# Second layer of a two-layer kernel: block-end sums on VectorE or preset in banks instead of on GpSimd, nine places for split inputs, first copies in another order

## The chip, the cores and the metric

The kernel runs on one core of a Trainium2 chip. The metric is the device time of one execution in microseconds (us). A core has a matrix engine (TensorE, PE in the rows), VectorE (DVE), ScalarE (ACT), GpSimd (POOL) and SyncE (SP), which here only starts DMA transfers. Each engine works through its own list in order, and waits on semaphores for the others.

## The reference, cut to what matters

```python
# q, k, v: (4, 8, 576, 64)
scores = scale * np.matmul(q, k.transpose(0, 1, 3, 2))
ret = scores * Dmat[None, :, :, :]              # decay by distance, zero above the diagonal
x = np.matmul(ret, v)                           # then (2304 tokens, 512)
# layer 1: w_in (512, 2048), w_out (2048, 512)
h = x @ w_in
x = (h * np.cos(h)) @ w_out
# layer 2: the same sizes
h = x @ w_in
g = np.where(h >= 1, h, np.where(h <= -1, 0.0, (h + 1) ** 2 / 4.0))
out = (g @ w_out).astype(np.float32)
```

The change touches the second layer, and the last three steps of the first.

## The kernel before, in words

**Tiling.** A float32 operand is split into a rounded high part and the rest, and a product is three passes over these parts (PASSES). The second layer also saves products: each of its two matrix products is cut into 2 by 2 pieces, and seven products of sums of pieces stand in for eight. The 2304 tokens come in three super-blocks of 768 (SB), two halves of 384 (TH). For each super-block there are four steps (NKB), each with a quarter of the 2048 hidden columns, so n counts 12 steps. A step has seven products for h (function products, and product for one) and then, one step later, seven groups for the output (function groups). A product or a group is 12 matmuls of 384 columns in two ops of 6, so a step has 168; the weights of one are one tile of 512 KB, loaded on SP's queue into a ring (function weight).

**Inputs.** The output of layer 1 lies in DRAM (yd). For a super-block, load_inputs fetches four quarter tiles q0 to q3. sum_q makes sums of them in place and in a fifth tile, and split_q makes the seven split inputs xc: ScalarE copies the high part, VectorE subtracts for the low part. In the order rows the tiles q0, q1, q2, q3 are q_4972, q_4974, q_4976, q_4978, and the fifth is q_5071. For the first super-block five of the seven are split while layer 1 still runs (EARLY), the other two after it (XEARLY). There are seven places for xc, one for each product, so the next super-block's copy waits for the last use of that product's place.

**PSUM.** Four double banks T0 to T3 (bkT in rows, pair_bank). Product 1 goes to T0; ScalarE copies T0 into T1 (seed, ACT bkT<-bkT), since products 6, 7 and 4 add to it there. T0 takes the place of layer 1's h banks, T1 that of its banks S and O. VectorE and ScalarE then make the curve g of what the banks hold, four combinations of the results (SUMS2), and seven splits into gh (ScalarE) and gl (VectorE, LOWS). A group's bank is added into an SBUF tile acc (DVE a<-bkT,a); in a super-block's first step ScalarE copies it there instead. The group at list index 5 of GPRODS (SEEDED) has, in all steps but the first, its acc copied into its bank first by ScalarE, and copied back after.

**Block end.** After the four steps of a super-block seven acc tiles are summed into four outputs and stored: six sums on GpSimd and one on VectorE (in the last super-block three and four).

**What sets the order.** The second layer's ops are listed with an engine, a cost, a position and their dependencies (op), and listed() plans the order of every engine's list: PE keeps the written order; every other engine takes, among the ops that are ready within 0.15 us of its earliest, the one of the lowest position. PE's planned clock starts at 0 and those of the other engines at -60, and a load is planned to land 6 us after it starts. So an op that needs nothing of the second layer's PE is planned before time 0, whatever its position. What is planned is fixed: an engine can't pass over an op that waits.

**Names.** In products, ORDER is the order of a step's products on PE (G: the first group of the step before). FIRST is the first step's: L0 and L1 are the last two parts of layer 1 (steps 78 and 79, mm2) and N is the next step's product 1. mm1 is layer 1's first matrix product, mm2 its second; a mm1 of 12 matmuls of 512 columns goes to a bank h, S or O.

Of the kernel before, what the change touches and what calls it, by code (L numbers as in the profile page):

```python
# [33 lines left out]
GPRODS = (1, 4, 2, 7, 5, 6, 3)  # L34
NKB = NQ // 2
EARLY = (0, 2, 3, 1, 4)
XEARLY = {5: 2, 6: 4}
# [5 lines left out]
SEEDED = (5,)  # L43
LOWS = {1: ("DVE", 16.8), 4: ("DVE", 31), 2: ("DVE", 34), 7: ("DVE", 36), 5: ("DVE", 39), 6: ("DVE", 45), 3: ("DVE", 47)}
SUMS2 = {7: ("DVE", 20.4), 5: ("DVE", 21.8), 6: ("DVE", 30), 3: ("DVE", 33)}
XPOS = (-31, -25, -19, -6, -11, 3.6, 1)
# [60 lines left out]
def retention_moe_kernel(ctx: ExitStack, tc: tile.TileContext, qk, kv, win1, wout1, win2, wout2, ktab, out):  # L107
# [490 lines left out]
    def mm1(s):  # L598
# [3 lines left out]
        aside = s - 6 + N1 % 2 if s >= N1 - 2 else s if l == NBLK - 1 and s % 2 and s < N1 - 3 else None  # L602
# [310 lines left out]
    def load_inputs(sb, pos):  # L913
        for j, (h, g) in enumerate(((0, 0), (1, 0), (1, 1), (0, 1))):
            def load(j=j, g=g, o=sb * SB + h * TH):
                if not sb:
                    qa[j][1] = home_early(f"q{j}", (2, TH))
                SY.dma_start(out=qa[j][1], in_=yd[:, 2 * g:2 * g + 2, o:o + TH])
            op("SP", "load", pos + j, load, (), (qa[j][0],))
# [10 lines left out]
    def split_q(eng, pos, k):  # L930
        p = PRODS[k][0]
        if p == 6:
            sum_q(eng, pos - 4, 0, 4, 0, ALU.subtract)
        if p == 3:
            sum_q(eng, pos - 4, 3, 3, 0, ALU.subtract)
        u = qa[{1: 0, 6: 0, 2: 3, 7: 1, 5: 4, 4: 2, 3: 3}[p]]
        hi, lo = ("x", k, 0), ("x", k, 1)
        op("ACT", "copy", pos, lambda: A.activation(xat(k)[:, 0], u[1], AF.Copy), (u[0],), (hi,))
        op("DVE", "wide", pos + 0.8, lambda: V.tensor_tensor(out=xat(k)[:, 1], in0=u[1], in1=f(xat(k)[:, 0]), op=ALU.subtract), (u[0], hi), (lo,))

    def inputs(sb):
        base = sb * NKB * T0
        load_inputs(sb, base - 50)
        sum_q("POOL", base - 40, 4, 1, 2, ALU.add)
        sum_q("POOL", base - 38, 1, 0, 1, ALU.subtract)
        for k, pos in enumerate(XPOS):
            split_q("POOL", base + pos, k)
# [64 lines left out]
    tmp = {t: home2(t, (2, TH)) for t in ("h1", "m5", "u2")}  # L1012
# [3 lines left out]
    def weight(key, src, pos):  # L1016
        n = len(ring)

        def load():
            j = n % 9  # L1020
            pool, tag = (wr, "wi") if j < 5 else (lp, f"w{j - 5}") if j < 7 else (wk, f"wo{j + 7}")
# [3 lines left out]
        ring.append(op("SP", "load", pos, load, (), (("w", n % 9),), ring[-1:]))  # L1025
        return "w", n % 9
# [12 lines left out]
    def product(n, k, b):  # L1039
        sb, kb = n // NKB, n % NKB  # L1040
        p, which, start = PRODS[k]
        which += which == 2 and n == 0
# [315 lines left out]
```

## Time and profile before

| | us |
|---|---|
| three runs | 846.33, 847.08, 850.20 |
| median | 847.08 |
| the profiled execution | 845.47 |
| its span, first to last instruction | 843.7 |
| PE busy | 812.3 (96%) |
| VectorE, ScalarE, GpSimd busy | 656.0, 525.2, 215.6 |
| second layer's first product starts | 466.8 |

The rows come from that one execution. A time of start counts from the span's start. A bracket at the end of a row gives the idle time ahead of the instruction and what ended it. PEclk is the granted TensorE clock as a share of 2.4 GHz; 0.50 is 1.2 GHz.

### The profile page before, as it was taken

The numbers are of one execution on the slowest core, as the hardware profiler recorded it, in microseconds if no ns is written. First come the engines' busy times: TensorE is split into PE (matmuls) and PEld (weight loads), VectorE is DVE, ScalarE is ACT, GpSimd is POOL, SyncE is SP. The second block draws the span as 40 slices with busy tenths as digits, with TensorE's granted clock in tenths as the row PEclk, the third lists the DMA queues.
The fourth block names the chain that finished last, engine by engine and source line by source line (L and its number), as shares of the span: only waits on it lengthen the run. The fifth ranks groups of instructions, "written<-read, shape, count | busy, mean of one in ns | idle before, by whom it ended". The sixth has DMA issues, their size and how long they took to land.

```text
span 843.7 us, 14794 instructions
## 1 busy us (share of the span) xinstructions
PE 812.3 (96%) x5549; PEld 729.5 (86%) x5550; DVE 656.0 (78%) x928; ACT 525.2 (62%) x866; POOL 215.6 (26%) x154
## 2 busy tenths in 40 slices
PE   7999999999999999999999999999999999899996
PEld 5788888887877777778777899999999999899996
DVE  7988787548889898888995475897964897954786
ACT  4788788655665654566656486685565675366560
POOL 2333222423425333324334200021500010500002
PEclk9999999999999999999999999999999999999999
DMA  8997999745989997678885797789878778788772
GB/s 342 393 371 289 347 342 322 275 150 188 318 278 330 327 353 271 229 281 308 324 286 203 257 331 256 252 272 307 265 248 255 252 248 253 250 252 254 256 233 75
DMA packets 78007, 232.92 MB, mean 276 GB/s; under 512 B 8304, under 2 KB 15088, under 8 KB 77936
## 3 DMA queue, kind: packets, MB, share of 16 engines
q1 hardware_dynamic: 77936, 231.98, 79.8%
q8 instruction: 44, 0.72, 0.3%
q14 instruction: 27, 0.22, 0.1%
HBM read 184.76 MB, written 47.19 MB: 275 GB/s over the span
## 4 chain that ended last, share of the span: by engine, by line
PE 38%; DVE 11%; ACT 3%; DMA 2%; issue 2%; POOL 0%; SPq 0%; DVEq 0%; ACTq 0%
PE bkT L124 36%; DVE a L124 3%; DVE gl L124 1%; DMA wq<-cw 1%; DVE cw L288 1%; ACT a L124 1%; DVE t L662 1%; DVE X L271 1%; DVE t L671 1%; PE bkS L608 1%; DMA raw<-in_win_dram 1%; DVE V L272 1%; PE bky L625 0%; DVE s L124 0%; DMA wi<-wd 0%
## 5 line engine op out<-in xcount | busy, mean ns | idle before, releaser
L124 PE MATMUL bkT<-xc,w 128*128 128x384 f32 x1008 | 183.8, 340 | 9.2 <-ACT bkT L124 9.2
L124 PEld LDWEIGHTS bkT<-xc,w 128*128 128x128 f32 x1008 | 179.2, 192 | 10.7 <-ACT bkT L124 10.5
L124 PE MATMUL bkT<-gh,w 128*128 128x384 f32 x672 | 170.4, 334 | 0.0
L608 PE MATMUL h<-xhl,wi 128*128 128x512 f32 (+1 forms) x576 | 139.4, 389 | 2.2 <-DVE t L671 2.1
L608 PEld LDWEIGHTS h<-xhl,wi 128*128 128x128 f32 x576 | 105.5, 188 | 26.4 <-DVE t L671 4.4
L684 POOL TENSOR_TENSOR gl<-t,gh 128x512 fp32r<-128x512 f32 (+1 forms) x57 | 80.7, 1417 | 163.8 <-ACT gh L679 102.2
L124 PEld LDWEIGHTS bkT<-gh,w 128*128 128x128 f32 x672 | 121.2, 188 | 0.0
L124 PE MATMUL bkT<-gl,w 128*128 128x384 f32 x336 | 112.2, 334 | 0.0
L623 PE MATMUL bky<-gh,wo 128*128 128x512 f32 x208 | 82.0, 394 | 0.8 <-ACT gh L679 0.8
L624 PE MATMUL bky<-gh,wo 128*128 128x512 f32 x208 | 81.1, 390 | 0.0
L625 PE MATMUL bky<-gl,wo 128*128 128x512 f32 x208 | 78.1, 393 | 2.5 <-POOL gl L684 2.5
L124 POOL TENSOR_TENSOR a<-a,a 128x768 f32<-128x768 f32 x15 | 34.5, 2302 | 138.7 <-DVE a L124 138.4
L679 ACT ACTIVATE gh<-t 128x512 fp32r<-128x512 f32 (+1 forms) x57 | 35.3, 620 | 54.3 <-DVE t L671 54.1
L124 PEld LDWEIGHTS bkT<-gl,w 128*128 128x128 f32 x336 | 63.1, 188 | 0.0
L124 POOL TENSOR_TENSOR q<-q,q 128x768 f32<-128x768 f32 x8 | 16.0, 2001 | 173.5 <-DVE xc L124 140.6
L124 DVE SCALAR_TENSOR_TENSOR a<-bkT,a 128x768 f32<-128x768 f32 x36 | 34.4, 955 | 31.2 <-ACT a L124 30.7
L124 DVE TENSOR_TENSOR a<-bkT,a 128x768 f32<-128x768 f32 (+1 forms) x55 | 51.4, 938 | 8.6 <-PE bkT L124 8.1
L124 PE MATMUL h<-xhl,wi 128*128 128x256 f32 (+1 forms) x288 | 52.1, 330 | 2.7 <-ACT hs L124 1.7
L666 ACT ACTIVATE t<-t 128x512 f32<-128x512 f32 (+1 forms) x56 | 34.8, 622 | 30.9 <-DVE t L662 30.8
L124 DVE TENSOR_TENSOR gl<-a,gh 128x768 fp32r<-128x768 f32 x48 | 53.1, 1122 | 0.5 <-ACT gh L124 0.5
L124 PEld LDWEIGHTS h<-xhl,wi 128*128 128x128 f32 x288 | 43.7, 189 | 8.6 <-ACT hs L124 1.9
L625 PEld LDWEIGHTS bky<-gl,wo 128*128 128x128 f32 x208 | 38.8, 188 | 12.9 <-POOL gl L684 4.9
(189 smaller groups left out, 1582.3 us busy)
## 6 DMA issues: line engine op xcount, KB each, us to landing
w<-wq SPq DMA_DIRECT2D x84, 512.0 KB, 4.5
w<-wv SPq DMA_DIRECT2D x84, 512.0 KB, 4.4
wi<-wd SPq DMA_DIRECT2D x48, 512.0 KB, 5.3
raw<-in_win_dram SPq DMA_DIRECT2D x32, 512.0 KB, 6.2
raw<-in_wout_dram SPq DMA_DIRECT2D x32, 512.0 KB, 5.3
qkv<-in_qk_dram SPq DMA_DIRECT2D x16, 512.0 KB, 7.7
qkv<-in_kv_dram SPq DMA_DIRECT2D x16, 512.0 KB, 8.6
wd<-wi SPq DMA_DIRECT2D x16, 512.0 KB, 6.2
```

The lines of the kernel that those rows point to most:

```text
L124: ins = fn(*args, **kw)
L271: V.scalar_tensor_tensor(out=X, in0=raw[:, :, 0].bitcast(U32), scalar=2.0 ** -52, in1=X, op0=ALU.mult, op1=ALU.mult)
L272: done.append(V.tensor_tensor(out=v, in0=W, in1=X, op=ALU.add))
L288: V.tensor_tensor(out=t[:, ks, 1], in0=u, in1=f(t)[:, ks, 0], op=ALU.subtract)
L608: lastpe[0] = PE.matmul(hp[s][:, :n], w[:, a, kb, :], x[b][:, kb, :], start=(i == 0), stop=(i == 3 * KB - 1))
L623: PE.matmul(o, w[:, 0, es], a, start=first and e % per == 0, stop=False, skip_group_check=True)
L624: PE.matmul(o, w[:, 1, es], a, start=False, stop=False, skip_group_check=True)
L625: PE.matmul(o, w[:, 0, es], b, start=False, stop=last, skip_group_check=True)
L662: V.scalar_tensor_tensor(out=t, in0=t, scalar=-MAGIC, in1=h, op0=ALU.add, op1=ALU.subtract)
L666: A.activation(u, u, AF.Sin, scale=TWOPI / 2)
L679: A.activation(gh[s], rt[s], AF.Copy)
L684: G.tensor_tensor(out=gl[s], in0=u, in1=f(gh[s]), op=ALU.subtract)
```

## The change

Eight things, all in or just ahead of layer 2:

1. The input sums (sum_q) of the second and third super-block move from GpSimd to VectorE.
2. The block-end sums: of seven, three are now made by presetting a group's bank with another acc (ENDS: groups 6 and 2 with acc 1, group 3 with acc 5; ScalarE, PSUM) and four by VectorE. GpSimd has no work left in layer 2.
3. The groups of products 3, 4 and 5 are preset with their own acc in a super-block's two middle steps, where before that of product 6 was in all steps but the first (SEEDED held list indices, and now holds product numbers); GPRODS and the positions LOWS, SUMS2 are new.
4. xc has nine places used in turn (NX) in place of seven.
5. The weight ring has seven tiles in place of nine: the sixth and seventh were in space of their own and are now where layer 1's last two weights (wo14, wo15) lie.
6. The tile h1 goes; its sum is made in m5's place.
7. The banks of layer 1's last mm1 are dealt otherwise: step 77 in S, 78 in h, 79 in O (before: h, S, S).
8. XPOS, SPOS, XEARLY and the q loads' positions are new.

```diff
@@ -34 +34 @@
-GPRODS = (1, 4, 2, 7, 5, 6, 3)
+GPRODS = (1, 5, 6, 2, 7, 3, 4)
@@ -35,0 +36,2 @@
+NX = 9
+SPOS = (-44, -42)
@@ -37 +39 @@
-XEARLY = {5: 2, 6: 4}
+XEARLY = {5: 6, 6: 8}
@@ -43,4 +45,6 @@
-SEEDED = (5,)
-LOWS = {1: ("DVE", 16.8), 4: ("DVE", 31), 2: ("DVE", 34), 7: ("DVE", 36), 5: ("DVE", 39), 6: ("DVE", 45), 3: ("DVE", 47)}
-SUMS2 = {7: ("DVE", 20.4), 5: ("DVE", 21.8), 6: ("DVE", 30), 3: ("DVE", 33)}
-XPOS = (-31, -25, -19, -6, -11, 3.6, 1)
+SEEDED = (3, 4, 5)
+ENDS = {6: 1, 2: 1, 3: 5}
+SEED_AT = 2
+LOWS = {1: ("DVE", 15), 5: ("DVE", 21), 6: ("DVE", 44), 2: ("DVE", 38.5), 7: ("DVE", 34), 3: ("DVE", 49), 4: ("DVE", 53)}
+SUMS2 = {7: ("DVE", 29), 5: ("DVE", 15), 6: ("DVE", 34), 3: ("DVE", 37.5)}
+XPOS = (-17, -20, -17.5, -4.4, -13, -4.5, -3.2)
@@ -602 +606 @@
-        aside = s - 6 + N1 % 2 if s >= N1 - 2 else s if l == NBLK - 1 and s % 2 and s < N1 - 3 else None
+        aside = None if l < NBLK - 1 else s if s % 2 else s + 1 if s == N1 - 1 else None
@@ -919 +923 @@
-            op("SP", "load", pos + j, load, (), (qa[j][0],))
+            op("SP", "load", pos + 5 * j, load, (), (qa[j][0],))
@@ -930 +934 @@
-    def split_q(eng, pos, k):
+    def split_q(eng, pos, k, sb=0):
@@ -933 +937 @@
-            sum_q(eng, pos - 4, 0, 4, 0, ALU.subtract)
+            sum_q(eng, pos - 2, 0, 4, 0, ALU.subtract)
@@ -935 +939 @@
-            sum_q(eng, pos - 4, 3, 3, 0, ALU.subtract)
+            sum_q(eng, pos - 2, 3, 3, 0, ALU.subtract)
@@ -937,3 +941,4 @@
-        hi, lo = ("x", k, 0), ("x", k, 1)
-        op("ACT", "copy", pos, lambda: A.activation(xat(k)[:, 0], u[1], AF.Copy), (u[0],), (hi,))
-        op("DVE", "wide", pos + 0.8, lambda: V.tensor_tensor(out=xat(k)[:, 1], in0=u[1], in1=f(xat(k)[:, 0]), op=ALU.subtract), (u[0], hi), (lo,))
+        x = (sb * 7 + k) % NX
+        hi, lo = ("x", x, 0), ("x", x, 1)
+        op("ACT", "copy", pos, lambda: A.activation(xat(x)[:, 0], u[1], AF.Copy), (u[0],), (hi,))
+        op("DVE", "wide", pos + 0.8, lambda: V.tensor_tensor(out=xat(x)[:, 1], in0=u[1], in1=f(xat(x)[:, 0]), op=ALU.subtract), (u[0], hi), (lo,))
@@ -943,3 +948,3 @@
-        load_inputs(sb, base - 50)
-        sum_q("POOL", base - 40, 4, 1, 2, ALU.add)
-        sum_q("POOL", base - 38, 1, 0, 1, ALU.subtract)
+        load_inputs(sb, base - 70)
+        sum_q("DVE", base + SPOS[0], 4, 1, 2, ALU.add)
+        sum_q("DVE", base + SPOS[1], 1, 0, 1, ALU.subtract)
@@ -947 +952 @@
-            split_q("POOL", base + pos, k)
+            split_q("DVE", base + pos, k, sb)
@@ -1012 +1017,2 @@
-    tmp = {t: home2(t, (2, TH)) for t in ("h1", "m5", "u2")}
+    tmp = {t: home2(t, (2, TH)) for t in ("m5", "u2")}
+    xplace.update((j, home2(f"xc{j}", (2, 2, TH), F32R)) for j in range(7, NX))
@@ -1020,2 +1026,2 @@
-            j = n % 9
-            pool, tag = (wr, "wi") if j < 5 else (lp, f"w{j - 5}") if j < 7 else (wk, f"wo{j + 7}")
+            j = n % 7
+            pool, tag = (wr, "wi") if j < 5 else (wk, f"wo{j + 9}")
@@ -1025,2 +1031,2 @@
-        ring.append(op("SP", "load", pos, load, (), (("w", n % 9),), ring[-1:]))
-        return "w", n % 9
+        ring.append(op("SP", "load", pos, load, (), (("w", n % 7),), ring[-1:]))
+        return "w", n % 7
@@ -1041,0 +1048 @@
+        x = (sb * 7 + k) % NX
@@ -1051 +1058 @@
-                    PE.matmul(o, w[:, u, h, :], xat(k)[:, v, h, :], start=start and i == h == 0, stop=i == 2 and h == 1, skip_group_check=True)
+                    PE.matmul(o, w[:, u, h, :], xat(x)[:, v, h, :], start=start and i == h == 0, stop=i == 2 and h == 1, skip_group_check=True)
@@ -1053 +1060 @@
-            op("PE", "PE", b + a, lambda a=a: run(a), (key, ("x", k, 0), ("x", k, 1)), (("T", which),))
+            op("PE", "PE", b + a, lambda a=a: run(a), (key, ("x", x, 0), ("x", x, 1)), (("T", which),))
@@ -1062 +1069 @@
-        m5, u2, h1 = [(x, tmp[x]) for x in ("m5", "u2", "h1")]
+        m5, u2 = [(x, tmp[x]) for x in ("m5", "u2")]
@@ -1086 +1093 @@
-                op("PE", "mm2", b + s, lambda j=j: steps_of(N1 - 2 + j, "M"), (("w", 7 + j),), (("last", j),))
+                op("PE", "mm2", b + s, lambda j=j: steps_of(N1 - 2 + j, "M"), (("w", 5 + j),), (("last", j),))
@@ -1108 +1115 @@
-                op("DVE", "wide", b + s - 2, lambda: V.tensor_tensor(out=h1[1], in0=b1[1](), in1=m5[1], op=ALU.add), (m5[0], b1[0]), (h1[0],))
+                op("DVE", "wide", b + s - 2, lambda: V.tensor_tensor(out=m5[1], in0=b1[1](), in1=m5[1], op=ALU.add), (b1[0],), (m5[0],))
@@ -1110 +1117 @@
-                curve(s + 0.6, "a22", h1)
+                curve(s + 0.6, "a22", m5)
@@ -1140,2 +1147,2 @@
-        def sum_of(eng, pos, to, frm):
-            two(eng, pos, (("a", to), acc[to]), (("a", to), acc[to]), (("a", frm), acc[frm]))
+        def sum_of(pos, to, frm):
+            two("DVE", pos, (("a", to), acc[to]), (("a", to), acc[to]), (("a", frm), acc[frm]))
@@ -1153 +1160 @@
-            seeded = kb > 0 and i in SEEDED
+            frm = ENDS[p] if ends and p in ENDS else p if kb and not ends and p in SEEDED else None
@@ -1159 +1166 @@
-                if m == 0 and not seeded:
+                if m == 0 and frm is None:
@@ -1166 +1173 @@
-                        PE.matmul(o, w[:, a, u, m * P:(m + 1) * P], g[:, a], start=not seeded and a == j == 0, stop=a == 1 and j == 2, skip_group_check=True)
+                        PE.matmul(o, w[:, a, u, m * P:(m + 1) * P], g[:, a], start=frm is None and a == j == 0, stop=a == 1 and j == 2, skip_group_check=True)
@@ -1170,3 +1177,5 @@
-                A.activation(bk[tile_][:, :, :TH], c[1], AF.Copy)
-            if seeded:
-                op("ACT", "copy", b - 2, seed, (c[0],), (("T", tile_),))
+                A.activation(bk[tile_][:, :, :TH], acc[frm], AF.Copy)
+            if frm is not None:
+                op("ACT", "copy", b - SEED_AT, seed, (("a", frm),), (("T", tile_),))
+            if ends and p in (7, 4):
+                sum_of(b - 3, p, {7: 6, 4: 7}[p])
@@ -1175 +1184 @@
-            if kb == 0 or seeded:
+            if kb == 0 or frm == p:
@@ -1177 +1186 @@
-            elif lastone and ends and p == 3:
+            elif lastone and ends and p == 4:
@@ -1180 +1189 @@
-                    store(b + 2 + m, 3, 0, 1, slice(m, m + 1))
+                    store(b + 2 + m, 4, 1, 0, slice(m, m + 1))
@@ -1185,3 +1194,2 @@
-            slow = "DVE" if lastone else "POOL"
-            if p == 1:
-                sum_of("POOL", b + 8, 6, 1)
+            if p == 7:
+                sum_of(b + 1, 3, 6)
@@ -1189,13 +1197,10 @@
-                sum_of("POOL", b + 6, 2, 1)
-                store(b + 9, 2, 0, 0)
-            elif p == 5:
-                sum_of("POOL", b + 3, 3, 5)
-            elif p == 6:
-                sum_of("DVE", b + 3, 3, 6)
-                sum_of(slow, b + 3.5, 7, 6)
-                sum_of(slow, b + 4, 4, 7)
-                sum_of(slow, b + 5, 7, 5)
-                store(b + 7, 4, 1, 0)
-                store(b + 8, 7, 1, 1)
-            elif p == 3 and not lastone:
-                store(b + 5, 3, 0, 1)
+                store(b + 4, 2, 0, 0)
+            elif p == 3:
+                store(b + 4, 3, 0, 1)
+                if lastone:
+                    sum_of(b + 3, 5, 7)
+                    store(b + 4, 5, 1, 1)
+            elif p == 4 and not lastone:
+                store(b + 5, 4, 1, 0)
+                sum_of(b + 4, 7, 5)
+                store(b + 7, 7, 1, 1)
```

**ScalarE, start of layer 2.** The rows after the last step of layer 1 (gh). Before, two copies for the first super-block, then the seed of T1:

```order
L679 ACTIVATE gh<-t 128x512
L124 ACTIVATE xc_5482<-q_4976 128x768
L124 ACTIVATE xc_5501<-q_4978 128x768
L124 ACTIVATE bkT_5534<-bkT_5509 128x2x384
L124 ACTIVATE u_5481<-bkT_5534 128x768
```

With the change:

```order
L683 ACTIVATE gh<-t 128x512
L128 ACTIVATE xc_5483<-q_4976 128x768
L128 ACTIVATE xc_5498<-q_4978 128x768
L128 ACTIVATE xc_5481<-q_4972 128x768
L128 ACTIVATE xc_5482<-q_5071 128x768
L128 ACTIVATE bkT_5536<-bkT_5511 128x2x384
L128 ACTIVATE u_5480<-bkT_5536 128x768
```

Two more copies, of q_4972 (q0) and of q_5071 (q1 + q2), stand ahead of the seed; they fill the two added places for the second super-block.

**SP's queue, at the same place.** A load waits for the readers of its tile, and what is behind it waits too. Before, the first step's seven weights, then the second super-block's q tiles:

```order
L124 DMA w_5493<-wq_117 128x1024
L124 DMA w_5495<-wq_118 128x1024
L124 DMA w_5497<-wq_117 128x1024
L124 DMA q_4974<-yd 128x2x384
L124 DMA q_4972<-yd 128x2x384
L124 DMA q_4976<-yd 128x2x384
L124 DMA q_4978<-yd 128x2x384
L124 DMA w_5542<-wq_117 128x1024
```

With the change five weights come first, then the q tiles, then the sixth weight and, behind a store of layer 1's output, the seventh:

```order
L128 DMA w_5494<-wq_117 128x1024
L128 DMA q_4974<-yd 128x2x384
L128 DMA q_4972<-yd 128x2x384
L128 DMA q_4976<-yd 128x2x384
L128 DMA q_4978<-yd 128x2x384
L128 DMA w_5544<-wq_118 128x1024
L128 DMA yd<-a_5478 128x512
L128 DMA w_5573<-wq_117 128x1024
```

The four q loads moved ahead of two weight loads.

**Block end.** In the first super-block GpSimd had six sums in a row (a_5478, a_5477, a_5476, a_5475, a_5474, a_5473, a_5472 are the acc tiles of products 1, 5, 6, 2, 7, 3 and 4 with the change, and of 1, 4, 2, 7, 5, 6 and 3 before):

```order
L124 TENSOR_TENSOR a_5473<-a_5473,a_5478 128x768
L124 TENSOR_TENSOR a_5476<-a_5476,a_5478 128x768
L124 TENSOR_TENSOR a_5472<-a_5472,a_5474 128x768
L124 TENSOR_TENSOR a_5475<-a_5475,a_5473 128x768
L124 TENSOR_TENSOR a_5477<-a_5477,a_5475 128x768
L124 TENSOR_TENSOR a_5475<-a_5475,a_5474 128x768
```

Meanwhile VectorE had low parts, its one sum, and then the last group's bank (a<-bkT):

```order
L124 TENSOR_TENSOR s_5465<-a_5468,s_5466 128x768
L124 TENSOR_TENSOR gl_5455<-a_5468,gh_5462 128x768
L124 TENSOR_TENSOR gl_5454<-a_5469,gh_5461 128x768
L124 TENSOR_TENSOR a_5472<-a_5472,a_5473 128x768
L124 TENSOR_TENSOR a_5472<-bkT_6680,a_5472 128x768
L124 TENSOR_TENSOR gl_5453<-s_5467,gh_5460 128x768
```

With the change (a_5472 is now product 4's, the last group):

```order
L128 TENSOR_TENSOR a_5474<-a_5474,a_5476 128x768
L128 TENSOR_TENSOR gl_5456<-s_5467,gh_5463 128x768
L128 TENSOR_TENSOR a_5475<-bkT_6619,a_5475 128x768
L128 TENSOR_TENSOR a_5473<-a_5473,a_5476 128x768
L128 TENSOR_TENSOR a_5474<-bkT_6648,a_5474 128x768
L128 TENSOR_TENSOR a_5472<-a_5472,a_5474 128x768
L128 TENSOR_TENSOR a_5473<-bkT_6646,a_5473 128x768
L128 TENSOR_TENSOR a_5472<-bkT_6684,a_5472 128x768
L128 TENSOR_TENSOR a_5474<-a_5474,a_5477 128x768
```

VectorE now has the four sums among its banks, and no low part stands between the last two of these.

## Rows read from the trace of the kernel before

**Rows 1.** The page's part 1: span; busy us, share, instructions.

```profile
span 843.7 us, 14794 instructions
PE 812.3 (96%) x5549; PEld 729.5 (86%) x5550; DVE 656.0 (78%) x928; ACT 525.2 (62%) x866; POOL 215.6 (26%) x154
```

**Rows 2.** What PE waited for: us in total, times, longest.

```profile
PE bkT L124 <- ACT bkT L124: 9.2, 3, 3.8
```

**Rows 3.** Timeline, first block end: start, duration, instruction, count, idle before.

```profile
603.42 9.99 POOL L124 TENSOR_TENSOR a<-a,a 128x768 f32<-128x768 f32 x4 [1.76 <-DVE a L124]
...
604.12 2.60 DVE L124 TENSOR_TENSOR gl<-a,gh 128x768 fp32r<-128x768 f32 x1
...
609.17 2.57 DVE L124 TENSOR_TENSOR a<-a,a 128x768 f32<-128x768 f32 x1
611.85 0.96 DVE L124 TENSOR_TENSOR a<-bkT,a 128x768 f32<-128x768 f32 x1
...
613.74 8.07 PE L124 MATMUL bkT<-xc,w 128*128 128x384 f32 x36 [3.85 <-ACT bkT L124]
```

**Rows 4.** Timeline of PE: after the first block end's wait, and at the second.

```profile
621.65 0.51 PE L124 MATMUL bkT<-gh,w 128*128 128x384 f32 x2
...
736.04 8.83 PE L124 MATMUL bkT<-xc,w 128*128 128x384 f32 x36 [3.85 <-ACT bkT L124]
744.71 0.51 PE L124 MATMUL bkT<-gh,w 128*128 128x384 f32 x2
```

**Rows 5.** Busy us by window: PE, PEld, DVE, ACT, POOL, then PEclk, DMA share, GB/s.

```profile
500.00:608.00 108.00, 108.00 (x625) 108.00 (x624) 88.47 (x92) 72.43 (x89) 16.90 (x8) 1.00 0.83 268
...
617.00:618.00 1.00, 1.00 (x5) 1.00 (x4) 0.02 (x1) 0.81 (x1) 0.00 (x0) 0.50 0.89 295
```

**Rows 6.** Timeline of PE where layer 2 starts.

```profile
461.39 0.39 PE L623 MATMUL bky<-gh,wo 128*128 128x512 f32 x1
...
464.12 2.88 PE L608 MATMUL bkS<-xhl,wi 128*128 128x512 f32 x12
...
473.35 2.36 PE L124 MATMUL bkT<-xc,w 128*128 128x384 f32 x12 [1.53 <-ACT bkT L124]
```

**Rows 7.** Timeline of the other engines there; last, q loads from issue to landing.

```profile
471.04 1.56 ACT L124 ACTIVATE xc<-q 128x768 fp32r<-128x768 f32 x2
471.90 2.33 DVE L124 TENSOR_TENSOR xc<-q,xc 128x768 fp32r<-128x768 f32 x2 [0.57 <-ACT xc L124]
472.50 0.79 ACT L124 ACTIVATE bkT<-bkT 128x768 f32<-128x768 f32 x1
...
473.38 1.23 SPq L124 DMA_DIRECT2D q<-yd  x2
...
477.44 3.76 POOL L124 TENSOR_TENSOR q<-q,q 128x768 f32<-128x768 f32 x2 [4.90 <-DMA q<-yd]
...
DMA to landing us min/median/max: 3.9/4.1/5.9
```

**Rows 8.** Groups of instructions, 480 to 600 us: count, busy us, mean ns, idle before.

```profile
L124 DVE TENSOR_TENSOR gl<-a,gh 128x768 fp32r<-128x768 f32 x17 | 15.9, 951 | 0.0
L124 DVE SCALAR_TENSOR_TENSOR a<-h,a 128x768 f32<-128x768 f32 x5 | 6.2, 1246 | 2.8 <-ACT a L124 2.8
L124 ACT ACTIVATE xc<-q 128x768 fp32r<-128x768 f32 x7 | 5.7, 835 | 1.7 <-PE bkT L124 1.7
```

**Rows 9.** Weight loads: count, KB, median us to landing, in 448 to 470 and 480 to 500.

```profile
w<-wq SPq DMA_DIRECT2D x7, 512.0 KB, 4.5
...
w<-wq SPq DMA_DIRECT2D x3, 512.0 KB, 9.0
```

**Rows 10.** Timeline of the tail, PE and VectorE.

```profile
835.34 1.83 DVE L124 TENSOR_TENSOR a<-a,a 128x768 f32<-128x768 f32 x2 [2.03 <-ACT a L124]
836.14 0.34 PE L124 MATMUL bkT<-gl,w 128*128 128x384 f32 x1
...
839.60 0.55 DVE L124 TENSOR_TENSOR a<-bkT,a 128x384 f32<-128x384 f32 x1
```

## The prediction

> **What bounds the kernel now.** I read the page's part 1 first: PE is busy for 96% of the span [rows 1], so an edit elsewhere pays only where it ends a wait of PE, or works after PE's end. Then PE's waits: in layer 2 it waits for one thing, ScalarE's seed of bank T1, three times, 9.2 us in all [rows 2]. The timeline places them: 1.53 us where layer 2 starts [rows 6], and 3.85 us at the ends of the first two super-blocks [rows 3, 4]. The rest of layer 2 has no idle PE: 108.00 of 108.00 us in 500 to 608, 625 matmuls, so 0.1728 us each [rows 5]. Last, the tail: PE ends at 836.14 + 0.34 = 836.48, VectorE at 839.60 + 0.55 = 840.15 [rows 10], the span at 843.7 [rows 1].
>
> **Block ends.** Where the first 3.85 us come from is to be seen in the timeline: four GpSimd sums run from 603.42 for 9.99 us, and a VectorE instruction with two SBUF operands takes 2.60 or 2.57 us under them [rows 3], against 0.951 elsewhere [rows 8]. So VectorE reaches the last group's bank only at 611.85; the seed must wait for that bank, and PE for the seed [rows 3]. The change takes GpSimd out. Three such stretched instructions cost 2.60 + 2.60 + 2.57 - 3 x 0.95 = 4.9 us [rows 3, 8] (the second 2.60 stands between the two shown), more than the wait. What is late next? VectorE gets more to do: by the order, 27 and 26 instructions between the seeds around the first block end (27 and 21 around the second), where GpSimd's were beside 27 and 26. At 0.95 us [rows 8] 27 need 25.7 us; a step of 168 matmuls lasts 29.0 us [rows 5]. Three presets of 0.8 us (as the seed, 0.79 [rows 7]) go to ScalarE, which has at most 30 instructions of some 0.84 [rows 8], 25 us, in such a step. Both fit, so I take both waits as gone.
>
> A wait also costs clock. After the first, 36 matmuls took 621.65 - 613.74 = 7.91 us, after the second 744.71 - 736.04 = 8.67 [rows 3, 4], where 36 x 0.1728 = 6.22; the granted clock was 0.50 in 617 to 618 [rows 5], the lower level, 1.2 GHz. So 1.69 and 2.45 us more. Block ends: -(3.85 + 1.69) - (3.85 + 2.45) = **-11.8 us** (bounds: -11.8, and 0 if VectorE is late anyway, see the rivals).
>
> **Start of layer 2.** Two things change. The last mm1 (step 79) goes to bank O and runs ahead of mm2 of step 77, not after it: 464.12 - 461.39 = 2.73 us earlier [rows 6], and so is all that hangs on it. By itself this would end the 1.53 us wait. But the order shows two more copies ahead of the seed on ScalarE, of q0 and of q1 + q2 for the second super-block, since their places 7 and 8 are free at once. They wait for loads that can't start earlier: q2's tile is read by the first super-block's split, which frees it at 473.38, where SP starts the load [rows 7]; with the change at 473.38 - 2.73 = 470.65. GpSimd's sum, which waited for it, began at 477.44, so it landed in 477.44 - 473.38 = 4.06 us [rows 7]; now at 474.71. Then VectorE's sum (0.95 [rows 8]), ScalarE's copy (0.83 [rows 8]), the seed (0.79) and 0.06 to PE (472.50 + 0.79 against 473.35 [rows 6, 7]): 477.34. PE is done with its work ahead of that at 473.35 - 1.53 = 471.82, as before, since only the order of the same matmuls changes. It waits 5.52 us in place of 1.53: **+4.0 us**. Bounds from the landing: 3.9 us to 5.9 [rows 7], so +3.8 to +5.8; I take the 4.06 of the same load at the same place. VectorE's three instructions more lie in time in which it has nothing else, since its next work needs PE.
>
> The Trainium skill, DMA: Bandwidth & Descriptors, section Anatomy of one DMA, gives (for transfers issued by GpSimd; here SP issues) 2.0 us plus the bytes at 436 GB/s; for 384 KB that is an estimate of 2.9 us, against the 4.06 of the row, and the sum would be 1.2 us lower by it. The row stands in a stretch of busy DMA and decides.
>
> This wait is longer than those of the block ends, so the lower clock should come too: 1.69 to 2.45 us as above, I take the mean, **+2.1**. After the 1.53 us none was lost: the next twelve matmuls took 2.36 us [rows 6].
>
> **Weights.** With seven tiles in place of nine a load starts when the product seven earlier is done, so six products or groups of 12 x 0.1728 = 2.07 us [rows 5], 12.4 us, ahead of its use. It lands in 4.5 us, in 9.0 in the busiest stretch [rows 9]. At the start the sixth and seventh wait for layer 1's last two steps; the seventh then has the four products 2, 5, 7 and N, 8.3 us, to land. I take nothing; bounds 0 and 9.0 - 8.3 = 0.7.
>
> **Last groups.** After the last step PE has seven groups and nothing between. Group 6 is preset from acc 1, so between group 1's end and group 6 VectorE must add 0.95, ScalarE copy 0.8: 1.8 with hand-offs, in the 2.07 us of group 5. If VectorE is in another instruction, up to 0.95 late: 0 to +0.8, **+0.3**.
>
> **Tail.** Before, 3.67 us pass from PE's end to VectorE's, because two pairs of sums (the first 1.83 for two [rows 10]) stand between the halves of the last bank. Now two sums and group 3's bank can run while PE has its last group, and two halves of 0.55 remain: 0.6 to 1.2 us after PE. What follows VectorE's end stays, 843.7 - 840.15 = 3.55. So 4.2 to 4.75 in place of 7.22: -2.5 to -3.0, **-2.6**.
>
> Free: h1 in m5's place (same instructions, m5 isn't written again until a step later), the presets of the middle steps (VectorE adds become ScalarE copies, both off PE's path: ScalarE is 72.43 of 108 us busy [rows 5]).
>
> **Sum.** -11.8 + 4.0 + 2.1 + 0.3 - 2.6 = -8.0 us. The profiled execution took 845.47; 837.5 by it. The median of the runs is 1.6 above it (847.08), so 839.1 for the median.
>
> **Rivals.**
> (a) VectorE is the bound at the block ends. For it: the 27 instructions leave 3 us of a step; the mean of one form in 480 to 600 was 1.25 [rows 8]. It decides from 29.0 / 27 = 1.07 us for the mean instruction: then the last group's bank is late as before. Against: what was stretched there lay under GpSimd. If both waits stay: 847.08 + 4.0 + 2.1 + 0.3 - 2.6 = 850.9, **slower**; if one goes, about 845.
> (b) The start costs nothing: the seed isn't held, because the loads land in time. PE then gains the 1.53 as well: -11.8 - 1.5 + 0.3 - 2.6 = -15.6, 831.5. Against: q2 would have to land by 471.82 - 0.06 - 0.79 - 0.83 - 0.95 = 469.2, before it can start.
> (c) Seven tiles are too few: where loads land later than the 12.4 us, PE waits at each weight; at the start 9.0 us [rows 9] against 8.3 already costs 0.7, with the clock up to 3. 840 to 845.
>
> **How the numbers follow.** My sum 0.68, (a) 0.14 (half of it both waits), (b) 0.06, (c) 0.12. Likeliest: 839.1. Its own range, with landing, clock, last groups and tail at their ends: -11.8 + 3.8 + 1.7 + 0 - 3.0 = -9.3 to -11.8 + 5.8 + 2.5 + 0.8 - 2.5 = -5.2, so 837.8 to 841.9. To hold 8 in 10 it must take in most of (c), one wait of (a) and the runs' own spread (0.75 below the median): 835 to 845.5. About 0.5%, 4.2 us, is what a measurement of this kernel can tell from no change. Faster by more (below 842.9): 0.61 of the sum's 0.68, (b), half of (c): 0.73. Within: 0.07 of the sum, half of (a), a quarter of (c): 0.17. Slower: (a) with both waits, and the part of (c) in which loads are late all through layer 2: 0.10.
>
> **What the profile after would show.** Right: POOL with nothing after layer 1; PE's wait for ACT bkT once, 5 to 6 us, near 472 to 477, with ScalarE's row ahead of the seed waiting for VectorE's q sum, and PEclk 0.50 behind it; no wait of PE at either block end and every gl at 0.95; about 4.5 us from PE's end to the span's. Wrong: PE waiting for ACT bkT at a block end (a), for DMA w (c), or not at all near 472 (b).

## The result, and the profile after

The changed kernel took 837.09 us (median of four, 834.37 to 838.97) against 846.71: a ratio of 0.9875, 95% interval 0.9835 to 0.9916. The profiled execution was the longest of the four, 838.97 us, against 845.47 for that of before; their spans are 837.2 and 843.7.

Busy time (page, part 1), then PE's waits for ScalarE's banks (us in total, times, longest), as [rows 1, 2]:

```profile
span 837.2 us, 14788 instructions
PE 811.9 (97%) x5549; PEld 729.6 (87%) x5550; DVE 642.5 (77%) x933; ACT 543.1 (65%) x893; POOL 166.9 (20%) x131
...
PE bkT L128 <- ACT bkT L128: 5.1, 2, 4.8
```

Three waits of 9.2 us have become one of 4.8 and one of 0.3. The timeline puts the 4.8 where layer 2 starts (as [rows 6, 7]; PE first, then ScalarE, VectorE, SP; last, the q loads from issue to landing):

```profile
463.90 2.88 PE L612 MATMUL bkO<-xhl,wi 128*128 128x512 f32 x12
...
469.35 2.24 PE L128 MATMUL bkT<-xc,w 128*128 128x384 f32 x12
...
479.13 4.21 PE L128 MATMUL bkT<-xc,w 128*128 128x384 f32 x12 [4.81 <-ACT bkT L128]
...
486.25 14.07 PE L128 MATMUL bkT<-xc,w 128*128 128x384 f32 x80
...
474.42 0.84 ACT L128 ACTIVATE xc<-q 128x768 fp32r<-128x768 f32 x1 [2.02 <-DMA q<-yd]
477.54 0.84 ACT L128 ACTIVATE xc<-q 128x768 fp32r<-128x768 f32 x1 [2.28 <-DVE q L128]
478.29 0.79 ACT L128 ACTIVATE bkT<-bkT 128x768 f32<-128x768 f32 x1
...
476.55 1.95 DVE L128 TENSOR_TENSOR q<-q,q 128x768 f32<-128x768 f32 x2 [2.51 <-DMA q<-yd]
...
DMA to landing us min/median/max: 3.2/3.3/4.3
```

The seed at 478.29 stands behind two copies that wait, one for a q load and one for VectorE's sum, which waits for q2's load. The windows at that wait and over the stretch of [rows 5] (busy us of PE, PEld, DVE, ACT, POOL; PEclk, DMA share, GB/s):

```profile
479.00:483.00 4.00, 3.87 (x12) 3.87 (x13) 2.20 (x3) 0.08 (x1) 0.00 (x0) 0.50 0.01 3
500.00:608.00 108.00, 108.00 (x623) 107.74 (x623) 85.02 (x95) 81.64 (x104) 0.00 (x0) 1.00 0.85 270
```

Behind the wait PE runs at 0.50, that is 1.2 GHz. From 479.13 to 486.25 it needs 7.12 us for what took 4.92 in the kernel before (473.35 to 478.27): 2.2 us.

The first block end: VectorE, PE's two products ahead of the bank T1, ScalarE's seed of it (as [rows 3]); then the group of low parts, which had a mean of 1122 ns over the whole kernel before:

```profile
607.79 0.95 DVE L128 TENSOR_TENSOR gl<-s,gh 128x768 fp32r<-128x768 f32 x1
...
613.73 0.96 DVE L128 TENSOR_TENSOR a<-bkT,a 128x768 f32<-128x768 f32 x1 [0.52 <-PE bkT L128]
...
613.53 10.58 PE L128 MATMUL bkT<-xc,w 128*128 128x384 f32 x60
...
615.81 0.80 ACT L128 ACTIVATE bkT<-bkT 128x768 f32<-128x768 f32 x1 [1.40 <-PE bkT L128]
...
L128 DVE TENSOR_TENSOR gl<-a,gh 128x768 fp32r<-128x768 f32 x48 | 45.2, 953 | 14.0 <-ACT gh L128 14.0
```

The matmuls run on without a bracket: PE needs T1 after 24 of them, 4.34 us after their start (605.55 to 609.89 in the kernel before), so at 617.87, and the seed is done at 616.61, 1.26 us ahead. By its bracket the seed waited for PE and not for VectorE, whose bank was done at 614.69. The tail, as [rows 10], with the group of PE that holds the wait for the last presets:

```profile
L128 PE MATMUL bkT<-gh,w 128*128 128x384 f32 x672 | 170.8, 335 | 0.3 <-ACT bkT L128 0.3
...
832.63 0.34 PE L128 MATMUL bkT<-gl,w 128*128 128x384 f32 x1
...
833.01 1.02 DVE L128 TENSOR_TENSOR a<-bkT,a 128x384 f32<-128x384 f32 x2 [0.48 <-PE bkT L128]
```

PE ends at 832.97, the span 4.23 us later; before it was 7.22.

To compare kernels I use two stretches of the profiled execution: **layer 2**, from its first product on PE to PE's end, and the **tail** from there to the span's end. What lies ahead of them, layer 1, has the same instructions in all kernels up to its last three products, and varies from execution to execution.

| kernel | layer 2 starts | layer 2 | tail | median, its kernel before beside it |
|---|---|---|---|---|
| before | 466.83 | 369.65 | 7.22 | 846.71 |
| changed | 469.35 | 363.62 | 4.23 | 837.09, 846.71 |
| e1 | 467.39 | 356.34 | 4.27 | 828.65, 845.48 |
| e2 | 465.12 | 357.57 | 7.01 | 831.65, 845.48 |
| e3 | 466.10 | 364.26 | 4.24 | 836.21, 845.48 |
| e4 | 465.57 | 366.84 | 7.19 | 844.84, 845.78 |
| e5 | 469.21 | 356.35 | 4.24 | 830.26, 845.48 |
| e6 | 467.44 | 369.55 | 7.21 | 845.51, 845.78 |
| e7 | 467.79 | 357.80 | 7.01 | 831.93, 845.78 |
| e8 | 464.03 | 359.00 | 7.17 | 835.58, 845.78 |
| e9 | 468.14 | 355.98 | 6.98 | 831.98, 846.94 |
| e10 | 465.78 | 364.32 | 4.20 | 835.69, 846.94 |

### The profile page after: what moved, and what is told of

Its sections match the earlier page's. It is cut to its first block, busy times and chain, and to the rows that moved or that the text cites. A ratio compares the mean times of both kernels' runs of the same rounds, so it can differ in the third digit from the quotient of the medians.

```text
span 837.2 us, 14788 instructions
## 1 busy us (share of the span) xinstructions
PE 811.9 (97%) x5549; PEld 729.6 (87%) x5550; DVE 642.5 (77%) x933; ACT 543.1 (65%) x893; POOL 166.9 (20%) x131
## 4 chain that ended last, share of the span: by engine, by line
PE 43%; DVE 6%; DMA 3%; ACT 2%; issue 1%; SPq 0%; POOL 0%; DVEq 0%; ACTq 0%
PE bkT L128 41%; DMA wi<-wd 2%; DVE cw L292 1%; DVE t L666 1%; DVE X L275 1%; DMA wq<-cw 1%; DVE t L675 1%; DVE V L276 1%; DMA q<-yd 0%; PE bky L128 0%; DMA wv<-tw 0%; PE bky L629 0%; DMA wv<-cw 0%; PE bkO L612 0%; PE h L612 0%
## 5 line engine op out<-in xcount | busy, mean ns | idle before, releaser
L128 PE MATMUL bkT<-xc,w 128*128 128x384 f32 x1008 | 180.9, 337 | 4.8 <-ACT bkT L128 4.8
L128 PEld LDWEIGHTS bkT<-xc,w 128*128 128x128 f32 x1008 | 176.8, 189 | 5.6 <-ACT bkT L128 5.5
L128 DVE TENSOR_TENSOR gl<-a,gh 128x768 fp32r<-128x768 f32 x48 | 45.2, 953 | 14.0 <-ACT gh L128 14.0
L128 DVE TENSOR_TENSOR a<-bkT,a 128x768 f32<-128x768 f32 (+1 forms) x46 | 43.0, 937 | 10.9 <-PE bkT L128 10.9
L627 PEld LDWEIGHTS bky<-gh,wo 128*128 128x128 f32 x208 | 39.0, 188 | 8.8 <-issue 0.5
L128 ACT ACTIVATE gh<-a 128x768 fp32r<-128x768 f32 x48 | 40.1, 836 | 8.8 <-PE bkT L128 8.4
```

The source lines that it names most:

```text
L128: ins = fn(*args, **kw)
L627: PE.matmul(o, w[:, 0, es], a, start=first and e % per == 0, stop=False, skip_group_check=True)
```

## Experiments: the start of layer 2

**e1, copies behind the seed.** In the planner of the changed kernel:

```diff
-        ready = [-60.0] * len(ops)
+        ready = [12.0 if o[0] in ("ACT", "DVE") and o[2] > 60 else -60.0 for o in ops]
```

> The changed kernel, with one number of the planner altered: no ScalarE or VectorE op of the second or third super-block is planned before 12 us after layer 2's start. So the copies of q0 and of q1 + q2 into the two added places stand behind the seed of T1. All work is kept. Theory (the 4.81 us wait where layer 2 starts comes only from the seed standing behind a copy that waits for q2's load): the seed follows PE's first product and the copies for the first super-block, 471.59 + 0.8 + 0.79 = about 473.2, ahead of PE's need at 474.32, so no wait there, no lower clock behind it: 4.81 + 2.2 (the matmuls from 479.13 to the next bkT run took 7.12 us in place of the 4.92 of the kernel before) = 7.0 us less than the changed kernel, about 830. Rival one (PE needs the load, or the copies, in any case): the wait only moves to a later product of the step and the time stays within 2 us of 837. Rival two (the lower clock has another cause than the wait): the wait goes, PEclk still shows 0.50 near 475 to 490, gain 4.8.

PE and ScalarE at the start, and the window behind it:

```profile
472.20 2.24 PE L128 MATMUL bkT<-xc,w 128*128 128x384 f32 x12
...
470.34 0.79 ACT L128 ACTIVATE bkT<-bkT 128x768 f32<-128x768 f32 x1
...
470.00:490.00 20.00, 20.00 (x110) 19.13 (x109) 12.92 (x15) 11.78 (x16) 0.40 (x1) 1.00 0.89 311
```

The seed follows the first two copies directly, there is no wait, the clock stays at 1.00, and layer 2 is 7.28 us shorter than in the changed kernel (7.0 expected). Nothing comes in place of the wait. The time is 0.9803 of before (0.9785 to 0.9822): this version beats both kernels.

**e5, seven places.** In the changed kernel:

```diff
-NX = 9
+NX = 7
```

> The changed kernel with NX = 7: seven places for the split inputs in place of nine, so the second super-block's copies wait for the first super-block's last use of a place. All else as changed. Theory (the two added places let two copies, one of which waits for q2's load, be planned ahead of the seed, and this is the start wait): the wait at the start goes, as in the kernel with the copies behind the seed; about 830, 7 us less than the changed kernel, unless the later copies come too late for the second super-block, where PE would then wait for them. Rival (the nine places are needed, or the wait has another cause): 4.8 us at the start stays, or waits for xc of 1 us and more show in the first step of the second and third super-block; 837 or more.

Layer 2 took 356.35 us, as in e1, and PE's one wait for a bank is the 0.3 at the end. So the two added places brought the start wait, and nothing that shows: the copies that then wait for a place are in time. Ratio 0.9817 (0.9791 to 0.9843).

**e4, the new banks alone.** In the kernel before:

```diff
-        aside = s - 6 + N1 % 2 if s >= N1 - 2 else s if l == NBLK - 1 and s % 2 and s < N1 - 3 else None
+        aside = None if l < NBLK - 1 else s if s % 2 else s + 1 if s == N1 - 1 else None
```

> The kernel before with one edit: the banks of layer 1's last products are dealt as in the changed kernel, so the last mm1 (bank O) runs ahead of the mm2 of step 77. Theory: PE's first product of layer 2, and ScalarE's first two copies and the seed with it, come some 2.7 us earlier against PE's second product, so the 1.53 us wait at the start goes and nothing takes its place; the two waits of 3.85 us at the block ends stay. From layer 2's first product to PE's end 369.65 - 1.5 = 368.1 us; the time 1.5 us less than before, about 844. Rival (PE waits for the load or for ScalarE at the start whatever the banks are): the 1.53 us stays, 845.5.

PE's waits, and the first block end:

```profile
PE bkT L124 <- ACT bkT L124: 7.6, 2, 3.8
...
610.64 7.86 PE L124 MATMUL bkT<-xc,w 128*128 128x384 f32 x36 [3.82 <-ACT bkT L124]
```

The 1.53 us are gone and the block ends are as they were. Layer 2 is 2.81 us shorter: 1.81 at the start (from its first product to its third PE takes 9.63 us in place of 11.44, so the wait of 1.53 had cost 0.28 more at its two ends), 0.93 of lower clock behind the block ends (7.70 and 7.95 us for the 36 matmuls, against 7.91 and 8.67), and 0.06 in the two waits. The time itself can't tell this from nothing: ratio 0.9994 (0.9969 to 1.0019), where 0.998 was expected.

**e6, seven weight tiles alone.** In the kernel before:

```diff
-            j = n % 9
-            pool, tag = (wr, "wi") if j < 5 else (lp, f"w{j - 5}") if j < 7 else (wk, f"wo{j + 7}")
+            j = n % 7
+            pool, tag = (wr, "wi") if j < 5 else (wk, f"wo{j + 9}")
...
-        ring.append(op("SP", "load", pos, load, (), (("w", n % 9),), ring[-1:]))
-        return "w", n % 9
+        ring.append(op("SP", "load", pos, load, (), (("w", n % 7),), ring[-1:]))
+        return "w", n % 7
...
-                op("PE", "mm2", b + s, lambda j=j: steps_of(N1 - 2 + j, "M"), (("w", 7 + j),), (("last", j),))
+                op("PE", "mm2", b + s, lambda j=j: steps_of(N1 - 2 + j, "M"), (("w", 5 + j),), (("last", j),))
```

> The kernel before with one edit: the weight ring has seven tiles in place of nine (the sixth and seventh lie where layer 1's last two weights were). Theory (a load needs 4.5 us, 9.0 in the busiest stretch, and seven tiles give 12.4): PE waits for no weight, nor is it slower; from layer 2's first product to PE's end 369.6 us as before, the time 845.5 within 2. Rival (seven are too few, and the changed kernel pays for it in places that its wait at the start hides): PE shows waits for DMA w, 0.7 to 3 us at layer 2's start or a little at many products; 846 to 850.

No wait of PE for a weight, and the waits of before to 0.04 us; layer 2 took 369.55 us, the ratio is 0.9998 (0.9979 to 1.0018).

## Experiments: the block ends

**e2, all sums of before on VectorE.** In the kernel before:

```diff
-            slow = "DVE" if lastone else "POOL"
+            slow = "DVE"
...
-                sum_of("POOL", b + 8, 6, 1)
+                sum_of("DVE", b + 8, 6, 1)
...
-                sum_of("POOL", b + 6, 2, 1)
+                sum_of("DVE", b + 6, 2, 1)
...
-                sum_of("POOL", b + 3, 3, 5)
+                sum_of("DVE", b + 3, 3, 5)
```

> The kernel before with one edit: the block-end sums of the first two super-blocks run on VectorE in place of GpSimd; no presets, no added places, old order of the first copies; the input sums stay on GpSimd. Theory (GpSimd's sums stretch VectorE's instructions with two SBUF operands from 0.95 to 2.6 us, and that alone makes the last group's bank late): the two waits of 3.85 us at the block ends and the lower clock behind them go although VectorE has more to do, 28 instructions in the step of the block end x 0.95 = 26.6 of 29.0 us; VectorE's rows there are 0.95 each; the 1.53 us at the start stays: 11.8 us less, about 835. Rival (VectorE is full at the block end, and only the presets on ScalarE make the room): waits of 2 to 4 us stay at both block ends, 843 to 847.

PE's waits, and the rows of VectorE around the last group's bank:

```profile
PE bkT L124 <- ACT bkT L124: 1.5, 1, 1.5
...
602.87 2.82 DVE L124 TENSOR_TENSOR a<-a,a 128x768 f32<-128x768 f32 x3 [0.16 <-ACT a L124]
605.61 0.95 DVE L124 TENSOR_TENSOR a<-bkT,a 128x768 f32<-128x768 f32 x1
```

Only the start wait is left, and layer 2 is 12.08 us shorter, where 11.8 was expected. The presets aren't needed for that: VectorE holds 28 instructions in that step.

**e3, the changed kernel with GpSimd back.** Its four sums of the first two super-blocks on GpSimd:

```diff
-            two("DVE", pos, (("a", to), acc[to]), (("a", to), acc[to]), (("a", frm), acc[frm]))
+            two("POOL" if sb < NSB - 1 else "DVE", pos, (("a", to), acc[to]), (("a", to), acc[to]), (("a", frm), acc[frm]))
```

> The changed kernel with one edit: the four block-end sums that VectorE makes in the first and second super-block run on GpSimd again; the three presets on ScalarE stay. Theory (sums on GpSimd stretch VectorE): while the four sums run on GpSimd (about 2.5 us each), VectorE's rows with two SBUF operands take 1.5 to 2.6 us, and PE waits at the block ends again, up to 3.85 us each with 1.7 to 2.5 of lower clock: up to 11.8 us more than the changed kernel, up to 849. If the sums fall where VectorE has room, the rows are stretched but the wait is shorter. Rival (the number of VectorE's instructions made the wait, not their stretch): VectorE has four fewer, so no wait, 837.

PE's waits, then GpSimd and VectorE at the first block end:

```profile
PE bkT L128 <- ACT bkT L128: 5.2, 2, 4.9
...
604.41 10.03 POOL L128 TENSOR_TENSOR a<-a,a 128x768 f32<-128x768 f32 x4 [135.31 <-DVE a L128]
...
608.45 1.73 DVE L128 TENSOR_TENSOR gl<-a,gh 128x768 fp32r<-128x768 f32 x1
610.11 0.94 DVE L128 TENSOR_TENSOR a<-bkT,a 128x768 f32<-128x768 f32 x1
610.98 1.74 DVE L128 TENSOR_TENSOR s<-a,s 128x768 f32<-128x768 f32 x1
612.64 0.94 DVE L128 TENSOR_TENSOR a<-bkT,a 128x768 f32<-128x768 f32 x1
```

The rows are stretched as I said, and PE waits for none of it: GpSimd's sums at a block end don't make the wait by themselves. My theory fell here in its simple form. What differs from the kernel before is what stands ahead of the last bank. Here one stretched row of 1.7 us stands between two banks. There, three in a row stand ahead of it: two low parts of 2.60 and a sum of 2.57 [rows 3]. That sum reads what GpSimd made of products 3 and 5, the third of its six sums and the first of the four in the row of 603.42. Taken by itself, with VectorE's two low parts and the seed that ends the wait:

```profile
603.42 2.49 POOL L124 TENSOR_TENSOR a<-a,a 128x768 f32<-128x768 f32 x1 [1.76 <-DVE a L124]
...
604.12 5.12 DVE L124 TENSOR_TENSOR gl<-a,gh 128x768 fp32r<-128x768 f32 x2
...
612.90 0.80 ACT L124 ACTIVATE bkT<-bkT 128x768 f32<-128x768 f32 x1 [6.47 <-DVE a L124]
```

GpSimd's sum ended at 605.91, but VectorE's sum began at 609.17, with no idle time ahead of it [rows 3]: it waited for the two low parts ahead of it in VectorE's list, not for GpSimd. The planner had put them there. It counts 2.15 us for a sum on GpSimd and 0.96 for an instruction on VectorE (COST), so two low parts fitted into the time until GpSimd's sum would be done. e7 and e8 take this apart.

**e7, one sum moved.** In the kernel before, GpSimd's sum of products 3 and 5, which VectorE's sum ahead of the last bank reads:

```diff
-                sum_of("POOL", b + 3, 3, 5)
+                sum_of("DVE", b + 3, 3, 5)
```

> The kernel before with one edit: of the six block-end sums on GpSimd in each of the first two super-blocks one, that of the acc tiles of products 3 and 5, runs on VectorE. VectorE's sum ahead of the last group's bank reads it, so the last bank no longer waits for GpSimd's third sum (which began near 605.9 and ended near 608.4); the planner then puts the two low parts that stood ahead of that bank behind it. Five sums stay on GpSimd and go on stretching VectorE's instructions with two SBUF operands to 1.7 to 2.6 us. Theory one (the wait came from the stretch as such): three instructions with two SBUF operands still stand between the last two banks, up to 2.6 us each, so 1 to 4 us of wait stay at both block ends; 840 to 845. Theory two (it came from the chain through GpSimd's sum, and from what the planner puts ahead of the bank because of it; the stretch fills time that VectorE has): no wait at the block ends though rows of 1.7 to 2.6 us are still seen there, 12 us less than before, about 833.

PE's waits; GpSimd, VectorE and the seed at the first block end:

```profile
PE bkT L124 <- ACT bkT L124: 1.5, 1, 1.5
...
605.56 7.31 POOL L124 TENSOR_TENSOR a<-a,a 128x768 f32<-128x768 f32 x3 [2.99 <-ACT a L124]
...
606.03 2.61 DVE L124 TENSOR_TENSOR a<-a,a 128x768 f32<-128x768 f32 x1
608.75 0.96 DVE L124 TENSOR_TENSOR a<-bkT,a 128x768 f32<-128x768 f32 x1
609.62 4.06 DVE L124 TENSOR_TENSOR gl<-a,gh 128x768 fp32r<-128x768 f32 x2
...
609.80 0.80 ACT L124 ACTIVATE bkT<-bkT 128x768 f32<-128x768 f32 x1 [2.44 <-DVE a L124]
```

The expectation has the wrong sum in "began near 605.9 and ended near 608.4": those are the times of GpSimd's fourth sum, and the one that VectorE reads had ended at 605.91. So the wait that the edit ends is not one for GpSimd. Both waits are gone all the same, with one instruction moved per block end, while five sums stay on GpSimd and VectorE's rows still take 2.61 and 4.06 for two. The time is 0.9854 of before (0.9825 to 0.9883). What the edit changed is the planned order: the two low parts now stand behind the bank, and one stretched row stands ahead of it. PE's two products began at 606.49 here, so it needs T1 at 610.83; the seed ends at 610.60, 0.2 us ahead.

**e8, that sum alone left on GpSimd.** The edits of e2 but the last; against e2:

```diff
-                sum_of("DVE", b + 3, 3, 5)
+                sum_of("POOL", b + 3, 3, 5)
```

> The kernel before with all block-end sums of the first two super-blocks on VectorE but one: that of the acc tiles of products 3 and 5, which VectorE's sum ahead of the last group's bank reads, stays on GpSimd. Theory one (the stretch is the cause): one GpSimd sum of 2.5 us stretches one or two rows by 0.8 to 1.6 us; no wait, or under 1 us; about 833. Theory two (the chain through this sum is the cause): VectorE's sum can't start before GpSimd's end, some 3.4 us after the bank of product 5 where VectorE itself needs 0.95; what the planner puts between decides, a wait of 0 to 2 us at each block end, 833 to 838.

GpSimd, VectorE and PE at the first block end:

```profile
599.81 2.49 POOL L124 TENSOR_TENSOR a<-a,a 128x768 f32<-128x768 f32 x1 [16.13 <-DVE a L124]
...
599.65 0.95 DVE L124 TENSOR_TENSOR gl<-a,gh 128x768 fp32r<-128x768 f32 x1
600.51 2.60 DVE L124 TENSOR_TENSOR s<-a,s 128x768 f32<-128x768 f32 x1
603.03 2.68 DVE L124 TENSOR_TENSOR a<-a,a 128x768 f32<-128x768 f32 x3
...
607.52 6.54 PE L124 MATMUL bkT<-xc,w 128*128 128x384 f32 x36 [0.45 <-ACT bkT L124]
```

A wait of 0.45 us at each block end, without lower clock (36 matmuls in 6.54). Here too VectorE didn't wait for GpSimd: GpSimd's sum ended at 602.30, and VectorE's sums began 0.73 us later, right behind the one stretched row. So one stretched row, with three sums between it and the last bank, costs 0.45 here; one stretched row ahead of the bank costs nothing in e7, where 0.2 us were left. Both theories allowed such a wait, so its size doesn't decide between them; the starts and ends of these rows do.

For the kernel before this gives an estimate. The seed ended at 612.90 + 0.80 = 613.70, and PE needed T1 at 609.89. With the three rows ahead of the bank at 0.95 each, 4.9 us less, the seed would have ended near 608.8, 1.1 us ahead of PE; with only the sum stretched, 3.3 us less, near 610.4, 0.5 late. So the 3.85 us took both: the stretch, and two low parts planned ahead of the bank. This split is worked out, not measured; no run moves the low parts alone, and e7's edit has the whole list planned anew.

**e9, two edits.** The kernel before with the edits of e4 and e7:

```diff
-        aside = s - 6 + N1 % 2 if s >= N1 - 2 else s if l == NBLK - 1 and s % 2 and s < N1 - 3 else None
+        aside = None if l < NBLK - 1 else s if s % 2 else s + 1 if s == N1 - 1 else None
...
-                sum_of("POOL", b + 3, 3, 5)
+                sum_of("DVE", b + 3, 3, 5)
```

> The kernel before with two edits: the one block-end sum of the acc tiles of products 3 and 5 on VectorE, and the new banks of layer 1's last products. Theory (these two carry the gain of layer 2; the presets, the added places, the ring and the other sums carry none of it): no wait of PE in layer 2, so from layer 2's first product to PE's end 356.0 us (the kernel with the one sum took 825.59 - 467.79 = 357.8, with 1.53 of wait), a tail of 7 us as before; 829 to 832, below the changed kernel by 5 to 7. Rival (the presets or added places are needed with the new banks): a wait of 1 us and more for ScalarE's seed, 833 and above.

PE at the start and at its end:

```profile
472.95 2.24 PE L124 MATMUL bkT<-xc,w 128*128 128x384 f32 x12
...
823.78 0.34 PE L124 MATMUL bkT<-gl,w 128*128 128x384 f32 x1
```

PE waits for no bank in layer 2, which takes 355.98 us (356.0 expected). The ratio is 0.9821 (0.9796 to 0.9845). What e1 has over it is the tail, 4.27 against 6.98.

**e10, the changed kernel again**, with no edit.

> The changed kernel once more, on the same chip. Theory (its layer 2 started 2.5 us later than that of the kernel before only by the spread of layer 1, whose instructions are the same up to the last three products): layer 2's first product starts between 464 and 469.4, as in the other kernels, and the wait of 4.8 us at the start, none at the block ends and 4.2 us of tail repeat; 835 to 838. Rival (the other order of the last products costs layer 1 the 2.5 us): 469 or later again.

PE's second product:

```profile
475.60 4.21 PE L128 MATMUL bkT<-xc,w 128*128 128x384 f32 x12 [4.85 <-ACT bkT L128]
```

Start wait, block ends and tail repeat, and layer 2 starts at 465.78, 3.6 us earlier than in the first profile of the same kernel: that late start was spread of layer 1. Ratio 0.9872 (0.9854 to 0.9890).

## Why the prediction was right, and where it wasn't

The forecast was 839.1 us, measured were 837.09, in the range and faster by more than 0.5%. By terms (us):

| term | predicted | measured | by |
|---|---|---|---|
| block ends | -11.8 | -11.8 | what is left of layer 2's -6.03; e2 -12.1, e7 -11.85 |
| start of layer 2, wait | +4.0 | +3.3 | 4.81 - 1.53 |
| lower clock behind it | +2.1 | +2.2 | 7.12 - 4.92 |
| weights | 0 | 0 (-0.1) | e6 |
| last groups | +0.3 | +0.3 | the group's wait |
| tail | -2.6 | -3.0 | 4.23 - 7.22 |
| sum | -8.0 | -9.0 | layer 2 -6.03, tail -2.99 |

- **Block ends.** The size was right, and so was the count (rival (a), VectorE full, didn't come: the seed was 1.26 us early). The step "three such stretched instructions cost 4.9 us, more than the wait" holds for these three rows, which stood ahead of the last bank. It was incomplete as a cause: stretched rows behind the bank (e7), or single ones between banks (e3), made PE wait for nothing. I should have asked why two low parts stood there. The planner had fitted them in beside GpSimd's sum, and they went behind the bank once that one sum was on VectorE (e7). The change took away both the stretch and this order, so the number held; that one moved sum would do doesn't follow from the prediction.
- **Start.** The mechanism was as put: two more copies ahead of the seed, one behind q2's load. Mis-sized was the landing. With layer 2 starting 2.52 us later than in the profile of before, the forecast issue of 470.65 is 473.17; VectorE's sum began at 476.55, so 3.38 us where I took 4.06. This gives a wait of 5.52 - 0.68 = 4.84; it was 4.81. The row of 4.06 stands in a stretch of busy DMA: the DMA share was 0.96 from its issue to its landing, and 1.03 from 470.00 to the issue. In the changed kernel, with the q loads ahead of two weight loads, these shares were 0.83 and 0.52. So the row was carried over to a place that had become quieter; that this made the landing faster isn't shown by a run. The Trainium skill, DMA: Bandwidth & Descriptors, section Anatomy of one DMA, led to an estimate of 2.9 us for these loads (for transfers that GpSimd issues); the 3.38 lies between it and the row.
- **The other side of this term** I didn't see: the prediction took the wait as the price of the added places. e1 shows that it is only an order, and e5 that the places bring nothing; without it the ratio is 0.9803 in place of 0.9875.
- **Tail.** 4.23 lies at the lower end of 4.2 to 4.75, in part by luck. VectorE ended 1.06 us after PE, inside 0.6 to 1.2, but what follows its end took 3.17 us (837.2 - 834.03) and not the same 3.55 as before. The reading of the kernel before was also off by one pair: of its two pairs of sums, one stood ahead of the first half of the last bank and only the other (1.94 us) between the halves.
- **The whole.** The sum fell short by 1.0 us. By the prediction's own working the profiled execution should have taken 837.5; it took 838.97, 1.0 less in layer 2 and the tail and 2.5 more in layer 1, which no term is about. That it stands beside the 839.1 that was meant for the median is chance. Over all profiles layer 2 started between 464.0 and 469.4, a spread larger than any term missed by.

## What to carry to other kernels

When an engine is late behind slow neighbours, look at which rows stand ahead of the late instruction in its own list, and ask why they were planned there, before you price the slowness. A stretched row costs only where it stands ahead of something that the bounding engine needs, and moving one instruction may clear that place and give all of the gain. To see whether an instruction waits for an operand or for its place in the list, compare its start with the end of what it reads and with the idle time ahead of it. Added buffers let a planner issue work early; check that none of this work waits for a load ahead of something that the bounding engine needs. And compare kernels stage by stage: parts that a change doesn't touch may vary by more than its terms.

## What the runs showed of the hardware

GpSimd and VectorE, both with two SBUF operands, took turns by whole instructions. In e8 GpSimd's sum began 0.16 us after a low part of VectorE and took 2.49 us, to 602.30 (in e7 a sum that began at 591.15, with no row of VectorE under way, took 1.84); VectorE's next sum, begun at 600.51, ended at 603.11, 0.81 after GpSimd's end. VectorE's rows that read a PSUM bank and one SBUF tile stayed at 0.94 beside GpSimd (e3), and between such rows the stretched ones took 1.74, not 2.6. The Trainium skill, SBUF — State Buffer, section SBUF: two separate sides, describes this as an exclusive lock that is held for a whole instruction; these rows agree.

The lower clock came behind waits of 3.81 to 4.90 us and not behind those of 0.45 and 1.53. What it cost didn't grow with the wait: 1.5 to 2.5 us behind 3.82 and 3.85, 2.2 behind 4.81.
